# A delta-rule attention with an MoE behind it: fewer unread products, other banks at the start, and a moved Gram step

## The chip, the cores and the metric

The kernel runs on one core of one Trainium2 chip. A core has TensorE (PE) for matrix products, VectorE (DVE), ScalarE (ACT) and GpSimd (POOL) for elementwise work, and SyncE (SP), which here issues the loads and stores. Each engine takes its instructions in the order written and waits on semaphores for the others. The metric is the device time of one execution in microseconds, the median of several runs; lower is better.

## The reference

For each of 4 x 8 heads a state of 48 x 48 is updated over 768 positions, and the outputs of all heads, side by side, go through a two-layer network with a softplus:

```python
k_n = k / (norm(k) + 1e-6)
for t in range(768):
    y[t] = q[t] @ state
    state += beta[t] * outer(k_n[t], v[t] - k_n[t] @ state)
h = x @ w_in                      # x: 3072 x 384, w_in: 384 x 2048
out = softplus(h) @ w_out         # w_out: 2048 x 384
```

## The kernel before

The positions are cut into 12 chunks of 64. Inside a chunk the recurrence is a triangular system, so a chunk needs the Gram matrix of its keys (`gram`), the inverse of a triangular matrix made from it (`invert`), and products with the state. Two chunks share one inversion `u`. `invert(u)` transposes the Gram blocks on DVE, makes norms (`norms`: DVE, ACT's Ln and Exp, small pieces on POOL), multiplies by a column and a row (lines 325 and 327, the two products), and then runs a loop of 30 pairs of a product and an addition (lines 339 and 343), for inversions 1 to 5 on POOL. `finish(u)` transposes the result back on DVE (lines 346 and 349).

Chunks 0 and 1 are done in another way, so that the network can start early: their inverse is left in blocks of 16, and `couple(s)` multiplies the strict blocks with it; its two PSUM banks are emptied into three tiles of `MT`, the third of which is the second bank with its halves swapped. `base` gives x0, `sweep` adds the coupling three times. For chunk 0 this stands in the prologue, before the first product of the network; `first_mask`, `first_u` and `first_y` make its output. `pairs` hands out the banks for x0 and the sweeps. `warm` writes products that nobody reads; their operand is a constant tile, and line 813 is theirs.

The network runs in passes of one or two chunks, cut into steps `t`: in step `t` PE does `hidden(i, g)` (line 691: 2 tiles of 128 hidden units), ACT and DVE the softplus, and one step later PE does `output(i, g)` (line 737). Pass 0 uses 32-bit weights, later passes split weights and activations into a high and a low part (`high` on ACT, `low` on DVE). The weights come as raw halves and are put together by `top` (ACT) and `convert` (DVE, line 648).

The order around the network is written by hand. `plan` holds blocks of attention work for step `t` (run on PE behind `hidden(t)`) or `t + 0.5` (behind the `output` that follows). A step's code is written out for all engines at once, and each engine keeps that order. `start(u, solver, due)` puts an inversion into a background list, from which `pull` takes pieces at later steps, at the latest in step `due`. GRAM, END, DONE and INV give these steps: gram(4) at 4, gram(5) and the start of inversion 2 at 7, due at 11.

Transfers are issued by SP in the order of the calls. In the prologue `load_q(1)` comes after `first_y(1)`, since it overwrites q, and behind it `feed(20)`: 20 halves of weights. At step 0 follow the keys `ki(1)`, at step 1 v of chunk 2 and the transposed keys `kT` of chunk 4 (`load_v(2)`, `load_k(4)`), which gram(4) reads.

Of the kernel before, what the change touches and what calls it, by code (L numbers as in the profile page):

```python
# [7 lines left out]
F32 = mybir.dt.float32  # L8
# [13 lines left out]
P = 128  # L22
# [9 lines left out]
N16 = 1  # L32
# [8 lines left out]
PASS = {s: i for i, p in enumerate(PASSES) for s in p}  # L41

STEPS = {2: (8, 8.5, 9, 9.5, 10.5, 11, 11), 3: (11.5, 12, 13, 13, 13.5, 14, 14)}
CLEAR, DONE, END, GRAM, INV = {}, {1: 8, 2: 19}, {1: 6, 2: 17}, {4: 4, 5: 7}, {2: 11}
CLEAR.update({2: 9, 3: 12})
Q_FIRST = (2, 4, 5, 6, 7, 8, 9, 10)
for c in range(4, NS, 2):
# [13 lines left out]
def deltanet_moe(ctx, tc, kT, qT, kI, vN, beta, wts, out, outT):  # L61
# [14 lines left out]
    def bank(shape):  # L76
        turns[0] += 1
        if turns[0] % 4 == 0 and not both[0]:
            return ps_o.tile(shape, F32, name="po2")
        return ps_a.tile(shape, F32, name="pa")  # L80
# [62 lines left out]
        nc.sync.dma_start(NV[s], vN[s])  # L143

    def scale_v(s):
        (nc.vector if s > 1 else nc.gpsimd).tensor_tensor(NV[s], NV[s], NN[s].unsqueeze(2).to_broadcast([P, NP, D]),
                                op=ALU.mult)

    def parity(t):
# [139 lines left out]
    def diagonal(t, blocks, n, r0, c0, nr, nc_, wide=(True, True)):  # L289

        apart = n if t is Z else n * (HB + 1)
        dims = [t.ap[0]] + ([(apart, len(blocks))] if len(blocks) > 1 else [])
        dims += [(HB if wide[0] else 0, nr), (1 if wide[1] else 0, nc_)]
        return bass.AP(t.tensor, t.offset + r0 * HB + c0, dims)

    def invert(u):

        n = QB if u < N16 else HB  # L300
        blocks = range(0, HB, n)
        lq = one.tile([P, HB, HB], F32, name="ltq")
        nc.vector.transpose(lq, LTD[u].rearrange("p q i -> p i q"))  # L303
        yield 2200
        nm = norms(u, lq)
        next(nm)
        m = len(blocks)
        sq = diagonal(lq, blocks, n, 0, 0, n, n)
        for b in blocks:
            o = lq[:, b:b + n, b:b + n]  # L310
            nc.gpsimd.affine_select(
                out=o, in_=o, compare_op=ALU.is_gt, fill=0.0, base=0,
                pattern=[[1, n], [-1, n]], channel_multiplier=0)
        yield 300
        cT, ncT = yield from nm

        engine, cost = (nc.gpsimd, 0) if u in ON_POOL else (nc.vector, 1)
        if m > 1:
            by_col, by_row = (bass.AP(v.tensor, v.offset, [v.ap[0], (n, m)] + w) for v, w in
                              ((ncT, [(0, n), (1, n)]), (cT, [(1, n), (0, n)])))  # L320
        else:
            by_col = ncT.unsqueeze(1).to_broadcast([P, n, n])
            by_row = cT.unsqueeze(2).to_broadcast([P, n, n])
        first = engine if u == N16 else nc.vector
        first.tensor_tensor(sq, sq, by_col, op=ALU.mult)
        yield 200 + n * n * m
        first.tensor_tensor(diagonal(Z, blocks, n, 0, 0, n, n), sq, by_row, op=ALU.mult)
        yield 200 + n * n * m
        if m > 1:
            nc.gpsimd.tensor_copy(bass.AP(Z.tensor, Z.offset, [Z.ap[0], (n, m), (HB + 1, n)]),  # L330
                                  cT.rearrange("p (a b) -> p a b", b=n))
        else:
            engine.tensor_copy(Z.rearrange("p a b -> p (a b)")[:, 0:HB * HB:HB + 1], cT)
        for j in range(n - 2, 0, -1):
            r = n - 1 - j
            o = tmp[:, 0:m * r * j]
            o = (o.rearrange("p (a r j) -> p a r j", a=m, j=j) if m > 1
                 else o.rearrange("p (r j) -> p r j", j=j))
            engine.tensor_tensor(o, diagonal(Z, blocks, n, j + 1, j, r, j, (True, False)),  # L339
                                 diagonal(lq, blocks, n, j, 0, r, j, (False, True)),  # L340
                                 op=ALU.mult)
            z = diagonal(Z, blocks, n, j + 1, 0, r, j)
            engine.tensor_tensor(z, z, o, op=ALU.add)  # L343
            yield cost * 2 * (160 + m * r * j)
# [23 lines left out]
    def negative(engine, o, x):  # L368
        if engine is nc.scalar:
            engine.activation(o, x, AF.Copy, scale=-1.0)  # L370
        else:
            engine.tensor_scalar(o, x, -1.0, None, op0=ALU.mult)

    def couple(s):

        pms = [bank([P, NP // 2, C]) for e in range(2)]
        for i, e, p, ab, t in quads:
            nc.tensor.matmul(pms[e][tk[ab], i, :], LF[tk[t], s, p, :], DT[s][tk[t], p, :],
                             start=True, stop=True)
        negative(nc.scalar, MT[s][0], pms[0])  # L380
        negative(nc.scalar, MT[s][1], pms[1])
        for h in range(2):
            negative(nc.scalar, MT[s][2][tk[h]], pms[1][tk[1 - h]])

    def quarters(to, i0, n, flip, left, right, es=(0, 1), ends=None):

# [421 lines left out]
    def warm(*columns, behind=None):  # L808

        r = even if behind is None else behind  # L810
        to = unread[0] if unread else bank([P, 512])
        for m in columns:
            nc.tensor.matmul(to[:, 0:m], even[:, 0:P], r[:, 0:m], start=True, stop=True)  # L813

    with tc.manual_schedule(engines={ET.PE, ET.DVE, ET.Activation, ET.Pool, ET.SP}):
# [69 lines left out]
        warm(512)  # L885
        pts.append(first_p(1))
        run(iv)
        warm(512, 512)
        lq = one.tile([P, 2, NP // 2, C], F32, name="ltq")
        MT[0] = [lq[:, 0], lq[:, 1], two.tile([P, NP // 2, C], F32, name="gh")]  # L890
        warm(384, behind=Z.rearrange("p a b -> p (a b)"))
# [8 lines left out]
                [P, 8, D]), op=ALU.mult)  # L900
        for k in range(4):
            first_mask(k // 2, k % 2)
        couple(0)

        def pairs(g):
            return ([bank([P, 4, D]) for e in range(2)] if g == 0 else
                    [ps_h.tile([P, 4, D], F32, name=f"ph{e}") for e in range(2)])

        for g in range(2):
            i, to = slice(4 * g, 4 * g + 4), pairs(g)  # L910
            base(0, to, 4 * g, 4)
            nc.vector.tensor_copy(x_swap[:, i], to[1])
            nc.vector.tensor_copy(x_base[:, 0, i], to[0])
            for h in range(2):
                nc.gpsimd.tensor_copy(x_base[tk[h], 1, i], x_swap[tk[1 - h], i])
        warm(128)
        top()
        for b in range(C // QB):
# [12 lines left out]
        for g in range(2):  # L931
            sweep(0, 2, tos[g], 4 * g, 4, ends=(False, True))
            first_u(g, tos[g])
        warm(256)
        first_y(0)
        warm(256)
        first_y(1)
        load_q(1)
        both[0] = False
# [91 lines left out]
                                            op=ALU.add)  # L1031
            load_v(3)

        at(0, 6000, first_state, bind(steps, iv, 2))
        at(0.5, 0, bind(steps, iv, 2))
        at(1, 1200, bind(couple, 1), bind(scale_v, 1), bind(run, iv))
        at(2, 2400, bind(masked_keys, 1, 0))
        at(3, 2400, bind(masked_keys, 1, 1))
        at(4, 0, second_base)
# [12 lines left out]
        for c in range(2, NS, 2):  # L1052
            u = c // 2
            if STEPS[c][0] == STEPS[c + 1][0]:
                at(STEPS[c][0], 0, bind(cross_both, u, True))
                at(STEPS[c][1], 920, bind(cross_both, u, False), bind(scale_v, c + 1))
            else:
                for s in (c, c + 1):
                    at(STEPS[s][0], 0, bind(cross_a, s))
                    at(STEPS[s][1], 920 * (s - c), bind(cross_b, s),  # L1060
                       *([bind(scale_v, s)] if s > c else []))
            for s in (c, c + 1):
                a, b, k0, k1, v, y, z = STEPS[s]
                at(CLEAR[s], 0, bind(arrange, s))
                if c > 2:
                    at(k0, 2400, bind(all_keys, s))
                    at(k0 + 0.5, 0, bind(other_masks, s))
                    at(k0 + 1, 2400)
                    at(v, 0, bind(gram_and_corrected, s + 4, s) if s + 4 < NS else
                       bind(corrected, s))  # L1070
                    at(y, 1700, bind(state_and_y, s))
                    continue
                at(k0, 2400, *([bind(masked_keys, s, 0)] if k0 < k1 else []))
                at(k1, 2400, bind(masked_keys, s, *((1,) if k0 < k1 else (0, 1))))
                at(v, 0, bind(corrected, s))
                at(y, 1700, bind(y_all, s))
                if y == z:
                    at(y, 0, bind(next_state, s))
                else:
                    at(y, 0, bind(next_state, s, (0,)))  # L1080
                    at(z, 0, bind(next_state, s, (1,)))
            at(END[u], 0, bind(start, u, end, DONE[u]))
            if u > 2:
                if u == 3:
                    at(GRAM[c], 0, bind(load_beta, u), bind(systems, u), bind(gram_pair, c))
                at(8 * (c - 2) - (12 if u == 3 else EARLY), 0, bind(start, u, invert, INV[u]))
            elif u > 1:
                at(GRAM[c], 0, bind(load_beta, u), bind(systems, u), bind(gram, c))
                at(GRAM[c + 1], 0, bind(gram, c + 1), bind(start, u, invert, INV[u]))

        late, over = None, 0
        for t in range(8 * NS):
# [94 lines left out]
```

## Time and profile before

| | |
|---|---|
| median of 3 runs | 563.67 us (562.72 to 564.19) |
| profiled execution | 562.74 us, of it the span 561.0 us |
| PE matmul | 539.0 us busy (96%) |
| DVE, ACT | 367.2 and 363.9 us (65% each) |
| POOL | 209.6 us (37%) |
| granted clock of PE, mean | 0.988 |

The span is the time from the first to the last instruction; what the profiled execution took beyond it lies around the program. A busy engine is not the bound by itself: of interest is which engine is waited for last in a stretch. [...]

### The profile page before, as it was taken

The numbers are of one execution on the slowest core, as the hardware profiler recorded it, in microseconds if no ns is written. First come the engines' busy times: TensorE is split into PE (matmuls) and PEld (weight loads), VectorE is DVE, ScalarE is ACT, GpSimd is POOL, SyncE is SP. The second block draws the span as 40 slices with busy tenths as digits, with TensorE's granted clock in tenths as the row PEclk, the third lists the DMA queues.
The fourth block names the chain that finished last, engine by engine and source line by source line (L and its number), as shares of the span: only waits on it lengthen the run. The fifth ranks groups of instructions, "written<-read, shape, count | busy, mean of one in ns | idle before, by whom it ended". The sixth has DMA issues, their size and how long they took to land.

```text
span 561.0 us, 17602 instructions
## 1 busy us (share of the span) xinstructions
PE 539.0 (96%) x7479; PEld 443.0 (79%) x7479; DVE 367.2 (65%) x660; ACT 363.9 (65%) x719; POOL 209.6 (37%) x365
## 2 busy tenths in 40 slices
PE   5788999899999999999999999999999999999997
PEld 3476768699987888877888888888887888888885
DVE  7858966999757857368747378747375737444434
ACT  5668685898677874756773757754557754454453
POOL 7125898119980179701886001886000000000000
PEclk9699999999999999999999999999999999999999
DMA  9919911223240132220122220031310030010001
GB/s 201 330 49 373 315 38 32 72 58 86 58 90 2 32 72 57 72 85 4 30 70 60 70 89 3 3 81 29 77 71 4 1 71 2 15 57 0 2 0 57
DMA packets 35502, 39.56 MB, mean 71 GB/s; under 512 B 22528, under 2 KB 25216, under 8 KB 35424
## 3 DMA queue, kind: packets, MB, share of 16 engines
q1 hardware_dynamic: 35280, 38.18, 24.2%
q8 instruction: 59, 0.97, 0.7%
q10 hardware_dynamic: 144, 0.26, 0.1%
q14 instruction: 19, 0.16, 0.1%
HBM read 31.55 MB, written 4.72 MB: 65 GB/s over the span
## 4 chain that ended last, share of the span: by engine, by line
PE 69%; POOL 16%; DVE 7%; DMA 3%; issue 2%; ACT 2%; ACTq 0%; DVEq 0%; POOLq 0%
PE po L737 29%; PE ph L691 27%; POOL Z L343 7%; POOL tmp L339 7%; PE pa L596 3%; PE pa L479 2%; DMA kt<-kT 2%; PE pa L439 2%; PE pa L565 1%; DMA big<-qT 1%; PE po L813 1%; DVE tt L349 1%; PE ph L577 1%; PE pa L577 1%; DVE a L668 1%
## 5 line engine op out<-in xcount | busy, mean ns | idle before, releaser
L691 PE MATMUL ph<-x,b 128*128 128x512 f32 (+1 forms) x576 | 166.2, 373 | 0.0
L696 ACT ACTIVATE a<-ph 128x512 f32<-128x512 f32 x96 | 57.4, 598 | 157.8 <-PE ph L691 153.2
L691 PE MATMUL ph<-x,a 128*128 128x512 f32 (+1 forms) x384 | 129.6, 374 | 2.4 <-DVE a L648 1.8
L703 DVE SCALAR_TENSOR_TENSOR a<-ph,a 128x512 f32<-128x512 f32 x88 | 60.4, 687 | 93.5 <-ACT a L698 93.2
L691 PEld LDWEIGHTS ph<-x,b 128*128 128x128 f32 x576 | 105.0, 188 | 19.4
L737 PE MATMUL po<-gh,b 128*128 128x512 f32 (+1 forms) x241 | 97.6, 405 | 1.4 <-DVE gh L705 1.4
L737 PE MATMUL po<-gh,a 128*128 128x512 f32 (+1 forms) x241 | 94.1, 390 | 0.0
L343 POOL TENSOR_TENSOR Z<-Z,tmp 128x30 f32<-128x30 f32 (+9 forms) x150 | 89.6, 597 | 11.8
L339 POOL TENSOR_TENSOR tmp<-Z,ltq 128x30 f32<-128x30 f32 (+9 forms) x150 | 86.5, 576 | 11.4
L691 PEld LDWEIGHTS ph<-x,a 128*128 128x128 f32 x384 | 72.0, 189 | 15.6 <-DVE a L648 2.2
L706 DVE TENSOR_TENSOR gl<-a,gh 128x512 fp32r<-128x512 f32 x88 | 66.4, 754 | 7.9 <-DVE gh L705 0.5
L737 PE MATMUL po<-gl,b 128*128 128x512 f32 (+1 forms) x241 | 69.4, 389 | 0.0
L698 ACT ACTIVATE a<-a 128x512 f32<-128x512 f32 x96 | 60.7, 632 | 3.1
L697 ACT ACTIVATE a<-a 128x512 f32<-128x512 f32 x96 | 60.6, 632 | 3.1
L737 PEld LDWEIGHTS po<-gh,b 128*128 128x128 f32 x241 | 45.2, 187 | 12.7 <-DVE gh L705 1.9
L737 PEld LDWEIGHTS po<-gl,b 128*128 128x128 f32 x241 | 45.2, 188 | 9.6
L737 PEld LDWEIGHTS po<-gh,a 128*128 128x128 f32 x241 | 45.3, 188 | 8.5
L705 DVE CAST gh<-a 128x512 fp32r<-128x512 f32 x88 | 40.0, 454 | 8.1 <-DVE a L703 0.9
L602 DVE TENSOR_TENSOR x<-pa,x 128x384 fp32r<-128x384 f32 x21 | 11.6, 554 | 38.1 <-ACT x L601 38.1
L256 POOL COPY ss<-ltq 128x32 f32<-128x32 f32 x6 | 1.4, 241 | 86.8 <-DVE ltq L303 86.8
L737 PE MATMUL po<-a,gh 128*128 128x384 f32 x96 | 33.5, 444 | 0.3 <-DVE gh L709 0.3
L493 DVE TENSOR_TENSOR big<-pa,maskP 64x256 f32<-64x256 f32 x66 | 27.8, 421 | 1.0
(220 smaller groups left out, 752.8 us busy)
## 6 DMA issues: line engine op xcount, KB each, us to landing
a<-wts SPq DMA_DIRECT2D x16, 383.8 KB, 7.5
b<-wts SPq DMA_DIRECT2D x16, 383.8 KB, 7.4
kt<-kT SPq DMA_DIRECT2D x24, 192.0 KB, 3.4
big<-qT SPq DMA_DIRECT2D x24, 192.0 KB, 4.0
nv<-vN SPq DMA_DIRECT2D x12, 384.0 KB, 3.7
ki<-kI SPq DMA_DIRECT2D x24, 192.0 KB, 3.3
outT<-ot SPq DMA_DIRECT2D x13, 256.0 KB, 2.3
x<-x SPq DMA_DIRECT2D x66, 32.0 KB, 2.0
```

What stands on the lines that cost most here:

```text
L339: engine.tensor_tensor(o, diagonal(Z, blocks, n, j + 1, j, r, j, (True, False)), diagonal(lq, blocks, n, j, 0, r, j, (False, True)), op=AL ...
L343: engine.tensor_tensor(z, z, o, op=ALU.add)
L493: nc.vector.tensor_tensor(be[tk[ab], ab, e, 4 * g:4 * g + 4, 0:C], pks[e][t, :, 0:C], maskP[t].unsqueeze(1).to_broadcast([C, 4, C]), op=AL ...
L596: nc.tensor.matmul(py[tk[ab], i, :], big[:, at + C:at + 2 * C], big[:, at:at + C], start=True, stop=True)
L691: nc.tensor.matmul(ph[:, j], weight(i, f, a, k * P, P), xr[b][k], start=(c == 0), stop=(c == len(terms) * NK - 1))
L696: nc.scalar.activation(a, ph, AF.Abs)
L697: nc.scalar.activation(a, a, AF.Exp, scale=-1.0)
L698: nc.scalar.activation(a, a, AF.Ln, bias=1.0)
L703: nc.vector.scalar_tensor_tensor(a, ph, 0.0, a, op0=ALU.max, op1=ALU.add)
L705: nc.vector.tensor_copy(hi_lo[0], a)
L706: nc.vector.tensor_tensor(hi_lo[1], a, hi_lo[0], op=ALU.subtract)
L737: nc.tensor.matmul(PO[i][h][:, c], l, r, start=(fs[j] == 0 and m == 0), stop=(fs[j] == NF - 1 and m == k - 1 and c != (cut and parts[0])))
```

## The change

It takes away three unread products and shortens a fourth; gives x0 and the sweeps of chunk 0 the banks of `ph` and `po` instead of `pa` and `ph`; lets DVE empty the second bank of couple(0) and puts the third copy behind x0; puts one copy of x0 on ACT; puts the two products of inversion 1 and the scaling of v(1) on DVE, the latter behind the products; puts two pieces of inversion 1 ahead of the first state; and in the tables puts gram(4) at 3.5 and the start of inversion 2 at 8.5.

```diff
--- before.py
+++ after.py
@@ -41,7 +41,7 @@
 PASS = {s: i for i, p in enumerate(PASSES) for s in p}
 
 STEPS = {2: (8, 8.5, 9, 9.5, 10.5, 11, 11), 3: (11.5, 12, 13, 13, 13.5, 14, 14)}
-CLEAR, DONE, END, GRAM, INV = {}, {1: 8, 2: 19}, {1: 6, 2: 17}, {4: 4, 5: 7}, {2: 11}
+CLEAR, DONE, END, GRAM, INV = {}, {1: 8, 2: 19}, {1: 6, 2: 17}, {4: 3.5, 5: 7}, {2: 11}
 CLEAR.update({2: 9, 3: 12})
 Q_FIRST = (2, 4, 5, 6, 7, 8, 9, 10)
 for c in range(4, NS, 2):
@@ -143,7 +143,7 @@
         nc.sync.dma_start(NV[s], vN[s])
 
     def scale_v(s):
-        (nc.vector if s > 1 else nc.gpsimd).tensor_tensor(NV[s], NV[s], NN[s].unsqueeze(2).to_broadcast([P, NP, D]),
+        nc.vector.tensor_tensor(NV[s], NV[s], NN[s].unsqueeze(2).to_broadcast([P, NP, D]),
                                 op=ALU.mult)
 
     def parity(t):
@@ -321,10 +321,9 @@
         else:
             by_col = ncT.unsqueeze(1).to_broadcast([P, n, n])
             by_row = cT.unsqueeze(2).to_broadcast([P, n, n])
-        first = engine if u == N16 else nc.vector
-        first.tensor_tensor(sq, sq, by_col, op=ALU.mult)
+        nc.vector.tensor_tensor(sq, sq, by_col, op=ALU.mult)
         yield 200 + n * n * m
-        first.tensor_tensor(diagonal(Z, blocks, n, 0, 0, n, n), sq, by_row, op=ALU.mult)
+        nc.vector.tensor_tensor(diagonal(Z, blocks, n, 0, 0, n, n), sq, by_row, op=ALU.mult)
         yield 200 + n * n * m
         if m > 1:
             nc.gpsimd.tensor_copy(bass.AP(Z.tensor, Z.offset, [Z.ap[0], (n, m), (HB + 1, n)]),
@@ -378,9 +377,12 @@
             nc.tensor.matmul(pms[e][tk[ab], i, :], LF[tk[t], s, p, :], DT[s][tk[t], p, :],
                              start=True, stop=True)
         negative(nc.scalar, MT[s][0], pms[0])
-        negative(nc.scalar, MT[s][1], pms[1])
-        for h in range(2):
-            negative(nc.scalar, MT[s][2][tk[h]], pms[1][tk[1 - h]])
+        negative(nc.scalar if s else nc.vector, MT[s][1], pms[1])
+
+        def rest():
+            for h in range(2):
+                negative(nc.scalar, MT[s][2][tk[h]], pms[1][tk[1 - h]])
+        return rest
 
     def quarters(to, i0, n, flip, left, right, es=(0, 1), ends=None):
 
@@ -885,7 +887,6 @@
         warm(512)
         pts.append(first_p(1))
         run(iv)
-        warm(512, 512)
         lq = one.tile([P, 2, NP // 2, C], F32, name="ltq")
         MT[0] = [lq[:, 0], lq[:, 1], two.tile([P, NP // 2, C], F32, name="gh")]
         warm(384, behind=Z.rearrange("p a b -> p (a b)"))
@@ -900,19 +901,20 @@
                 [P, 8, D]), op=ALU.mult)
         for k in range(4):
             first_mask(k // 2, k % 2)
-        couple(0)
+        rest = couple(0)
 
         def pairs(g):
-            return ([bank([P, 4, D]) for e in range(2)] if g == 0 else
-                    [ps_h.tile([P, 4, D], F32, name=f"ph{e}") for e in range(2)])
+            return [(ps_o, ps_h)[g == 0].tile([P, 4, D], F32, name=f"{'po' if g else 'ph'}{e}")
+                    for e in range(2)]
 
         for g in range(2):
             i, to = slice(4 * g, 4 * g + 4), pairs(g)
             base(0, to, 4 * g, 4)
             nc.vector.tensor_copy(x_swap[:, i], to[1])
-            nc.vector.tensor_copy(x_base[:, 0, i], to[0])
+            copies[g](x_base[:, 0, i], to[0])
             for h in range(2):
                 nc.gpsimd.tensor_copy(x_base[tk[h], 1, i], x_swap[tk[1 - h], i])
+        rest()
         warm(128)
         top()
         for b in range(C // QB):
@@ -931,9 +933,8 @@
         for g in range(2):
             sweep(0, 2, tos[g], 4 * g, 4, ends=(False, True))
             first_u(g, tos[g])
-        warm(256)
+        warm(192)
         first_y(0)
-        warm(256)
         first_y(1)
         load_q(1)
         both[0] = False
@@ -1031,9 +1032,8 @@
                                             op=ALU.add)
             load_v(3)
 
-        at(0, 6000, first_state, bind(steps, iv, 2))
-        at(0.5, 0, bind(steps, iv, 2))
-        at(1, 1200, bind(couple, 1), bind(scale_v, 1), bind(run, iv))
+        at(0, 6000, bind(steps, iv, 2), first_state, bind(steps, iv, 2))
+        at(1, 1200, lambda: couple(1)(), bind(run, iv), bind(scale_v, 1))
         at(2, 2400, bind(masked_keys, 1, 0))
         at(3, 2400, bind(masked_keys, 1, 1))
         at(4, 0, second_base)
@@ -1086,7 +1086,8 @@
                 at(8 * (c - 2) - (12 if u == 3 else EARLY), 0, bind(start, u, invert, INV[u]))
             elif u > 1:
                 at(GRAM[c], 0, bind(load_beta, u), bind(systems, u), bind(gram, c))
-                at(GRAM[c + 1], 0, bind(gram, c + 1), bind(start, u, invert, INV[u]))
+                at(GRAM[c + 1], 0, bind(gram, c + 1))
+                at(8.5, 0, bind(start, u, invert, INV[u]))
 
         late, over = None, 0
         for t in range(8 * NS):
```

On PE, around steps 3 and 4, `ph` rows are the network's hidden products, `po_1026` and `po_1023` its outputs, `kt_74` the transposed keys of chunk 4, `nv` the products of second_base. Before:

```order
L737 MATMUL po_1027<-a_138,gh 128x384
L691 MATMUL ph_1134<-x_89,a_783 128x256 x3
L691 MATMUL ph_1134<-x_89,a_787 128x256 x3
L393 MATMUL pa<-nv,tt 64x48 x32
L192 MATMUL po_1190<-kt_74 64x64 x2
L192 MATMUL pa<-kt_74 64x64 x2
...
L737 MATMUL po_1026<-a_775,gh 128x384
```

and in the changed kernel:

```order
L739 MATMUL po_1024<-a_138,gh 128x384
L192 MATMUL pa<-kt_74 64x64 x32
L693 MATMUL ph_1177<-x_89,a_780 128x256 x3
L693 MATMUL ph_1177<-x_89,a_784 128x256 x3
L395 MATMUL po_1192<-nv,tt 64x48 x2
L395 MATMUL pa<-nv,tt 64x48 x2
...
L739 MATMUL po_1023<-a_772,gh 128x384
```

The Gram products of chunk 4 stood behind hidden(0, 4) and second_base and now stand ahead of both, directly behind output(0, 2).

On DVE, between the last weight part of step 7 (`a_1566`, `a_1563`) and the next step, `ltq<-work` is the transpose that begins inversion 2, `r`, `nt`, `ncT` and `nn` its norms, and `a<-ph` the softplus of step 8. Before:

```order
L668 TENSOR_TENSOR a_1566<-a_130,b_1503 128x768
L303 STREAM_TRANSPOSE ltq<-work 128x1024
L257 TENSOR_SCALAR rt<-ltq 128x32
L261 RECIPROCAL r_1603<-rt 128x32
L262 TENSOR_TENSOR r_1603<-r_1603,ss 128x32
L263 SCALAR_TENSOR_TENSOR nt<-r_1603,rt 128x32
L265 TENSOR_TENSOR r_1603<-nt 128x32
L266 RECIPROCAL r_1603<-r_1603 128x32
L269 SCALAR_TENSOR_TENSOR ncT<-r_1603,bet 128x32
L279 STREAM_TRANSPOSE nn<-nt 128x32
L285 TENSOR_SCALAR nn<-nn 128x32
L703 SCALAR_TENSOR_TENSOR a<-ph_1576,a 128x512
```

and in the changed kernel:

```order
L670 TENSOR_TENSOR a_1563<-a_130,b_1500 128x768
L705 SCALAR_TENSOR_TENSOR a<-ph_1573,a 128x512
L707 CAST gh<-a 128x512
L708 TENSOR_TENSOR gl<-a,gh 128x512
L670 TENSOR_TENSOR a_1638<-a_134,b_1502 128x768
L670 TENSOR_TENSOR a_1640<-a_138,b_1569 128x768
L670 TENSOR_TENSOR a_1642<-a_772,b_1571 128x768
L303 STREAM_TRANSPOSE ltq<-work 128x1024
L257 TENSOR_SCALAR rt<-ltq 128x32
L485 TENSOR_TENSOR nv<-nv,pa 128x4x48
```

The transpose stood ahead of the softplus of step 8 and now stands behind it and behind three weight parts; the norms follow later still, directly ahead of the two products of inversion 2, which keep their place ahead of the softplus of step 10.

## Rows read from the trace of the kernel before

**Rows 1.** The page's 40 slices: granted clock of PE, in tenths

```profile
PEclk9699999999999999999999999999999999999999
```

**Rows 2.** PE's waits: releaser, us in total, times, longest

```profile
PE ph L691 <- DVE a L648: 1.8, 1, 1.8
```

**Rows 3.** Timeline of the prologue: start us, us, engine, line, operation, tiles

```profile
25.05 0.92 ACT L364 ACTIVATE tt<-tmp,blk 128x256 f32<-128x256 f32 x2
25.42 1.98 PE L813 MATMUL po<-gl 128*128 128x512 f32 x4
27.98 1.16 PE L378 MATMUL pa<-tt,x 64*64 64x64 f32 x64
29.24 1.09 ACT L370 ACTIVATE ltq<-pa 128x512 f32<-128x512 f32 x2 [3.27 <-PE pa L378]
30.34 1.20 ACT L370 ACTIVATE gh<-pa 64x512 f32<-64x512 f32 x2
31.58 0.68 PE L393 MATMUL pa<-x,ltq 64*64 64x48 f32 x32
...
38.30 0.70 PE L813 MATMUL po<-gl 128*128 128x256 f32 x2
40.45 2.86 PE L691 MATMUL ph<-x,a 128*128 128x256 f32 x12 [0.60 <-ACT x L546]
```

**Rows 4.** SP's issues; loads from 38 to 76 us; us to landing from 61.1

```profile
39.87 1.31 SPq L135 DMA_DIRECT2D big<-qT  x2
61.20 4.18 SPq L127 DMA_DIRECT2D kt<-kT  x4
...
DMA packets 5301, 10.31 MB, mean 271 GB/s; under 512 B 2160, under 2 KB 2160, under 8 KB 5296
...
kt<-kT SPq DMA_DIRECT2D x1, 192.0 KB, 9.8
```

**Rows 5.** Timeline of PE around steps 3 and 4

```profile
66.38 2.75 PE L691 MATMUL ph<-x,a 128*128 128x256 f32 x12
...
71.18 0.30 PE L192 MATMUL po<-kt 48*64 48x64 f32 x2 [0.97 <-DMA kt<-kT]
...
72.90 2.85 PE L737 MATMUL po<-a,gh 128*128 128x384 f32 x8
```

**Rows 6.** PE's timeline, then stretches (PEclk: third from the end)

```profile
7.49 0.68 PE L177 MATMUL po<-kt 48*64 48x64 f32 x31
19.70 2.58 PE L192 MATMUL pa<-kt 48*64 48x64 f32 x64 [2.88 <-DMA kt<-kT]
...
11.00:11.50 0.50, 0.00 (x0) 0.00 (x0) 0.50 (x1) 0.00 (x0) 0.00 (x0) 0.89 1.33 246
25.00:25.50 0.50, 0.50 (x33) 0.43 (x25) 0.50 (x3) 0.50 (x3) 0.00 (x0) 0.96 1.04 418
```

**Rows 7.** Timeline of POOL and DVE, products of inversion 1 and a conversion

```profile
51.48 2.67 POOL L325 TENSOR_TENSOR ltq<-ltq,ncT 128x1024 f32<-128x1024 f32 x1
...
51.85 2.70 DVE L648 SCALAR_TENSOR_TENSOR a<-a,ex 128x384 int32<-128x384 int32 x1
57.26 0.54 DVE L648 SCALAR_TENSOR_TENSOR a<-a,ex 128x384 int32<-128x384 int32 x1
```

**Rows 8.** Timeline of ACT and DVE, steps 8 to 10

```profile
103.64 0.63 ACT L698 ACTIVATE a<-a 128x512 f32<-128x512 f32 x1
...
103.58 1.95 DVE L303 STREAM_TRANSPOSE ltq<-work 128x1024 f32<-128x1024 f32 x1
106.31 0.35 DVE L261 RECIPROCAL r<-rt 128x32 f32<-128x32 f32 x1 [0.56 <-ACT rt L259]
108.53 0.68 DVE L703 SCALAR_TENSOR_TENSOR a<-ph,a 128x512 f32<-128x512 f32 x1
121.75 1.23 DVE L327 TENSOR_TENSOR Z<-ltq,cT 128x1024 f32<-128x1024 f32 x1
```

**Rows 9.** Timeline of POOL and PE: end of loop 2, wait behind finish(2)

```profile
166.91 0.27 POOL L343 TENSOR_TENSOR Z<-Z,tmp 128x30 f32<-128x30 f32 x1
...
173.15 0.50 PE L737 MATMUL po<-gh,b 128*128 128x512 f32 x1 [0.56 <-DVE gh L705]
```

## The prediction

> **What bounds the kernel now.** The page comes first: PE fills its slices and its clock is up from 28 us on [rows 1], so time can be won only where PE stands still or does work that nobody reads. The table of PE's waits shows where it stands, behind weight conversions on DVE above all [rows 2], behind late keys and a few copies. I then read the timeline in PE's order, because PE takes its work strictly as written and hands a late start on to all that follows.
>
> In the first 40 us PE, ACT and DVE work as a chain. The coupling runs at 27.98, its last copy is out of ACT only at 31.54, the first sweep starts at 31.58, and the first MoE product, after ACT's copy of y, at 40.45 [rows 3]. From 40 us on a second thing runs: a stream of loads. SP starts it at 39.87 when the last first_y has read q, and the keys of chunk 4 stand at its end: issued at 61.20, landed 9.8 us later, about 71.0 [rows 4]. PE asks for them at 71.18 after waiting 0.97 us [rows 5]. After that PE hardly waits until 173.15, where gh is late by 0.56 us [rows 9]: gh stands behind finish(2) on DVE, and that behind the last step of POOL's second loop, at 167.18 (166.91 + 0.27). So two things set the end: when the keys of chunk 4 arrive, and when POOL's second loop starts.
>
> **The prologue.** Without the two unread 512-wide products, couple(0) waits only for ACT's masks, which end at 25.97 (25.05 + 0.92) [rows 3], and for the unread product behind Z, which then ends near 26.2: couple starts 1.8 us earlier. Its two halves are then emptied side by side: ACT takes 0.55 (half of 1.09) [rows 3]. DVE has no row for such a copy; the nearest are ACT's 0.55 and its own softplus, as wide and also out of PSUM, 0.68 [rows 8]. I take 0.68; one mask that is late on DVE would add 0.5. The third copy (1.20) moves behind x0, and since x0 and the sweeps have other banks, its bank no longer holds the first sweep. That sweep then starts near 28.7 (couple done at 27.3, DVE's copy, behind its masks, until 28.3, a copy of x0 0.35) instead of 31.58: 2.9 us. Before first_y(1) an unread 256-wide product of 0.70 goes [rows 3]; the copy of u on ACT hides some of it, which leaves 0.45. Sum: the first MoE product, and with it the start of the load stream, comes 3.3 us earlier (36.5 for the stream). Bounds 1.8 (only the unread product counts) and 3.9.
>
> **The second inversion's start.** Its two 1024-wide products on POOL took up to 2.67 us, and one of DVE's conversions beside them took 2.70 instead of about 0.55 [rows 7]; PE waited 1.8 us for a conversion [rows 2]. On DVE they are two instructions like the later inversion's 1.23 [rows 8], and they now stand behind those conversions. So PE's wait of 1.8 goes, and 0.3 of the following wait for gh. POOL's first loop starts about 6 us earlier; PE and DVE reach the place where it is read later than it ends, so those 6 us are slack and count nothing. The same holds for scale_v(1) on DVE (0.9): DVE has room there because its conversions are no longer stretched; if that cover went, keys(1) would be 0.9 late.
>
> **gram(4) moved ahead.** PE used to end output(0, 2) at 66.38 [rows 5]. With 3.3 + 1.8 + 0.3 taken off it ends at about 61.0, and now the next thing in PE's row is gram(4), which needs the keys. These come with the stream. SP's order of loads is unchanged, the weights before the keys keep the engines full, so the keys shift by the stream's start only: 71.0 - 3.3 = 67.7. PE therefore stands still for 6.7 us (bounds 5.5 and 7.5). Behind gram(4) wait hidden(0, 4), second_base and output(0, 3); ACT, DVE and POOL have nothing that can use the time.
>
> What is then late: before, gram took from 71.18 to 72.90 (1.72) and output(0, 3) followed; hidden(0, 4) and second_base, 3.83 us (71.18 - 0.97 - 66.38), were already done [rows 5]. Now they come after the keys. Shift at the start of output(0, 3) (72.90 before): -3.3 + 3.8 = +0.5 us. The whole prologue gain and the removed waits are spent here.
>
> **The clock.** PE's long run ends at 8.17 in the first gram; with only a fraction of a microsecond of work in between, the granted clock goes from 1.00 to 0.50 in the slice from 11.00, and it is back in the slice from 25.00, after PE worked from 19.70 on [rows 6]. [...] A stop of 6.7 us is longer than what went before that fall, so I expect PE to restart at the low level. If it stays there as long as from 19.70 to 25.02, 5.3 us, gram takes 2.58 as it did there instead of 1.72, 0.9 more, and hidden(0, 4) loses half of the 2.7 that are left, 1.3: together 2.2. Bounds 0 (no fall) and 3.5 (7 us at the low level). I take 2.2. The shift is then +2.7 at output(0, 3), and PE, which hardly waited from there to step 8, carries it along.
>
> **The third inversion's start.** Before, DVE did its transpose from 103.58 and its norms until 108.53, then softplus(8) and all else, and the second product ended at 122.98 (121.75 + 1.23) [rows 8]. So ACT's end of softplus(8), 104.27, stood 18.7 before the loop. Now softplus(8) and three weight parts come first, and transpose and norms later, in the same row of DVE: 14.45 (122.98 - 108.53) plus the 4.95 that were between 103.58 and 108.53, less the wait for ACT in it, 0.56 [rows 8], is 18.84, some 18.9 from ACT's end. DVE idles before ACT's end instead of using that time. Costs 0.2, bounds 0 and 0.8. That ACT no longer holds cross_a's copies behind the logarithm saves PE about 1.6 at step 8, but PE only arrives earlier at the wait of 173.15; this counts nothing.
>
> **The sum.** POOL's second loop starts -3.3 + 3.8 + 2.2 + 0.2 = +2.9 us later. Its length (44.2, from 122.98 to 167.18) I leave, with 1 us either way for DVE's traffic. finish(2) follows at once, PE waits for it, and everything behind shifts by 2.9. The profiled execution took 562.74 (span 561.0 and 1.74 around it), so 565.6 on its account; it lies 0.9 below the median of 563.67, so the median of the runs should be 566.5.
>
> [...] The stream's length is the step on which all hangs. The trace has 10.31 MB at a mean of 271 GB/s from 38 to 76 us [rows 4], and PE waited for its end.
> [...]
>
> **The rivals.** *The keys don't hold PE* (12%). If keys and PE arrive together at 61, PE is 6.4 us early at output(0, 3) (72.90 against 61.0 + 1.72 + 3.83 = 66.5), POOL's second loop starts at most 5.8 earlier (finish(1) and the steps behind it on DVE take the rest): 557.9. It takes a stream that ends at 61; the result turns at about 66.6 with the clock up (where -3.3 + 3.8 + 0.2 becomes 0). For it: the last megabyte moves at half the rate of the weights, so there is room. Against it: nothing in that part of the queue is changed, and the issue of each load waits for the eighth before it.
>
> *PE stops but its clock stays up, or comes back at once* (20%). Then +0.7: 564.4, no change that can be told. For it: PE stood 1.8 us in one place [rows 2] and the clock row shows 9 in every slice from 28 us on [rows 1]. Against: 6.7 us is nearly four times that, and the fall in rows 6 came 3.3 us after the last long run.
>
> *The clock falls in the prologue too* (8%). The unread products are what fills PE between 25.4 and 40; if one of the new gaps lets the clock fall there, the small products of about 10 us run at half rate, some 4 us later, and the stream with them: 570.5. For it: three stretches of filling go. Against: the chain gets shorter by as much, and no gap of over 1 us opens.
>
> *The forecast* (60%): 566.5, own range 565 to 568.5.
>
> **Numbers.** A measurement of this kernel can't tell less than 0.3%, 1.7 us, from no change. Faster: the first rival, and a little of the second, 0.13. Same: most of the second and the low end of the forecast, 0.27. Slower: 0.60. The range from 562.0 to 569.5 leaves out the first rival and half of the third.
>
> **What would show it.** In the changed profile: couple(0) near 26.2 and the first MoE product near 37.1; no long conversions beside POOL; PE idle about 6.7 us before gram's first product, released by the key load; granted clock 0.50 for about five us after it; POOL's second loop starting near 125.9; PE waiting over 2 us for gh at about 176. I am wrong if PE finds the keys landed, if the clock stays at 1.00, or if the wait at finish(2) isn't there.

## The result and the profile after the change

The changed kernel takes 568.16 us, median of six executions (566.1 to 569.59), where the kernel before took 563.22 on the same chip: ratio 1.0083, 95% interval 1.0058 to 1.0108, so 4.9 us slower by the medians and 4.7 by the ratio. The forecast was 566.5, 2.8 above the median it started from. The profiled execution has a span of 567.1 us, before 561.0. Its checkpoints, in us from the span's start:

| | before | forecast | after |
|---|---|---|---|
| couple(0) starts | 27.98 | 26.2 | 26.14 |
| first sweep | 31.58 | 28.7 | 30.70 |
| first MoE product | 40.45 | 37.1 | 40.02 |
| stream of loads starts | 39.87 | 36.5 | 39.39 |
| gram(4) gets its keys | 71.18 | 67.7 | 69.78 |
| PE's wait just before | 0.97 | 6.7 | 5.68 |
| output(0, 3) starts | 72.90 | 75.6 | 78.06 |
| third inversion's second product done | 122.98 | 125.9 | 128.07 |
| PE's product behind finish(2) | 173.15 | 176 | 179.03 |

The prologue comes first: the timeline of the changed kernel, its PE, ACT, DVE and SP rows (columns as in [rows 3] and [rows 4]).

```profile
26.14 1.16 PE L377 MATMUL pa<-tt,x 64*64 64x64 f32 x64
27.39 0.60 ACT L369 ACTIVATE ltq<-pa 128x512 f32<-128x512 f32 x1 [1.62 <-PE pa L377]
27.41 0.68 DVE L371 TENSOR_SCALAR ltq<-pa 128x512 f32<-128x512 f32 x1
27.57 0.51 PE L395 MATMUL po<-nv,tt 64*64 64x48 f32 x18
29.91 0.44 PE L395 MATMUL po<-nv,tt 64*64 64x48 f32 x14 [1.83 <-issue]
30.70 0.68 PE L395 MATMUL ph<-x,ltq 64*64 64x48 f32 x32
40.02 2.86 PE L693 MATMUL ph<-x,a 128*128 128x256 f32 x12 [0.57 <-ACT x L548]
39.39 1.31 SPq L135 DMA_DIRECT2D big<-qT  x2
60.33 4.40 SPq L127 DMA_DIRECT2D kt<-kT  x4
```

Coupling, and its emptying by two engines, came as forecast, to 0.2 us, the DVE copy at the 0.68 that was taken for it. Then base's second half stops after 18 of its 32 products for 1.83 us, and the releaser is "issue": no semaphore that the profile knows. Of the 3.3 us of the forecast 0.4 reach the first MoE product.

PE around the keys of chunk 4, which answers to [rows 5]:

```profile
61.25 2.85 PE L739 MATMUL po<-a,gh 128*128 128x384 f32 x8
69.78 2.46 PE L192 MATMUL pa<-kt 48*64 48x64 f32 x64 [5.68 <-DMA kt<-kT]
72.16 4.89 PE L693 MATMUL ph<-x,a 128*128 128x256 f32 x12
78.06 2.85 PE L739 MATMUL po<-a,gh 128*128 128x384 f32 x8
```

Three stretches of the same kernel (bounds, length, busy time of PE, PEld, DVE, ACT, POOL, then granted clock as a share of PE's full speed, DMA share, GB/s):

```profile
30.00:35.00 5.00, 5.00 (x156) 4.32 (x158) 2.74 (x10) 2.12 (x6) 0.69 (x2) 0.69 0.03 7
65.00:70.00 5.00, 0.23 (x2) 0.26 (x2) 3.94 (x6) 0.00 (x0) 4.53 (x7) 0.95 0.88 210
70.00:75.00 5.00, 4.97 (x71) 4.12 (x71) 0.00 (x0) 2.62 (x8) 4.45 (x8) 0.50 0.03 8
```

PE stands still for the keys, and the granted clock behind that is 0.50: gram takes 2.46 us and hidden(0, 4) 4.89. It was down in the prologue too: two us after the stop in base it fell, and from 32 to 34 us it was 0.50.

The third inversion and the end of its loop, on ACT, DVE and POOL, and PE behind it (these answer to [rows 8] and [rows 9]):

```profile
108.79 0.63 ACT L700 ACTIVATE a<-a 128x512 f32<-128x512 f32 x1
109.45 0.69 DVE L705 SCALAR_TENSOR_TENSOR a<-ph,a 128x512 f32<-128x512 f32 x1 [4.58 <-ACT a L700]
114.10 2.07 DVE L303 STREAM_TRANSPOSE ltq<-work 128x1024 f32<-128x1024 f32 x1
126.84 1.23 DVE L326 TENSOR_TENSOR Z<-ltq,cT 128x1024 f32<-128x1024 f32 x1
133.70 0.74 PE L418 MATMUL pa<-tt,off 32*32 32x32 f32 x64 [1.97 <-DVE x L606]
172.07 0.27 POOL L342 TENSOR_TENSOR Z<-Z,tmp 128x30 f32<-128x30 f32 x1
179.03 0.50 PE L739 MATMUL po<-gh,b 128*128 128x512 f32 x1
```

From ACT's end of softplus(8), 109.42, to the second product's end are 18.65 us, where 18.9 was forecast. POOL's second loop starts and ends 5.1 us late, and PE's product behind it 5.9. The long wait for gh that was expected at 176 is missing: PE itself came late, since it waited 1.97 us at 131.7 for a bank that DVE empties behind the norms of the third inversion.

### The profile page after: what moved, and what is told of

It is laid out like the page before. It is cut to its first block, busy times and chain, and to the rows that moved or that the text cites. A ratio compares the mean times of both kernels' runs of the same rounds, so it can differ in the third digit from the quotient of the medians.

```text
span 567.1 us, 17588 instructions
## 1 busy us (share of the span) xinstructions
PE 542.2 (96%) x7473; PEld 446.5 (79%) x7473; DVE 365.4 (64%) x663; ACT 363.6 (64%) x719; POOL 202.6 (36%) x362
## 4 chain that ended last, share of the span: by engine, by line
PE 85%; DMA 6%; DVE 3%; ACT 2%; SPq 1%; issue 1%; POOL 1%; ACTq 0%; DVEq 0%; POOLq 0%
PE po L739 33%; PE ph L693 33%; PE pa L598 4%; DMA kt<-kT 3%; DMA b<-wts 3%; PE pa L481 2%; PE pa L441 2%; PE pa L567 2%; PE pa L579 1%; PE pa L192 1%; PE ph L579 1%; PE ph L241 1%; PE po L395 1%; PE po L815 1%; DMA big<-qT 1%
## 5 line engine op out<-in xcount | busy, mean ns | idle before, releaser
L693 PE MATMUL ph<-x,a 128*128 128x512 f32 (+1 forms) x384 | 132.1, 383 | 0.6 <-ACT x L548 0.6
L693 PEld LDWEIGHTS ph<-x,b 128*128 128x128 f32 x576 | 106.3, 191 | 19.4
L338 POOL TENSOR_TENSOR tmp<-Z,ltq 128x30 f32<-128x30 f32 (+9 forms) x150 | 85.0, 567 | 11.4
L693 PEld LDWEIGHTS ph<-x,a 128*128 128x128 f32 x384 | 74.2, 194 | 13.9 <-ACT x L548 0.7
```

Source lines behind the costliest of these rows:

```text
L693: nc.tensor.matmul(ph[:, j], weight(i, f, a, k * P, P), xr[b][k], start=(c == 0), stop=(c == len(terms) * NK - 1))
```

## The experiments

Each ratio is to the kernel before, run on the same chip (its medians were 563.0 to 563.2).

| kernel | us | ratio | 95% interval |
|---|---|---|---|
| the change | 568.16 | 1.0083 | 1.0058 to 1.0108 |
| a_gram_behind | 565.59 | 1.0045 | 1.0031 to 1.0059 |
| b_gram_ahead | 566.35 | 1.0058 | 1.0044 to 1.0071 |
| a_fill | 565.93 | 1.0060 | 1.0036 to 1.0083 |
| a_keys_early | 559.66 | 0.9942 | 0.9926 to 0.9957 |
| a_warm_kept | 567.69 | 1.0082 | 1.0061 to 1.0102 |
| a_keys_feed_less | 558.01 | 0.9914 | 0.9901 to 0.9928 |
| a_inv3_at7 | 565.01 | 1.0042 | 1.0027 to 1.0057 |
| a_pool_products | 567.69 | 1.0084 | 1.0062 to 1.0107 |
| best7 | 558.02 | 0.9918 | 0.9898 to 0.9938 |
| b_keys_feed_less | 562.38 | 0.9992 | 0.9979 to 1.0005 |

The ratio is not the quotient of the two medians. a_gram_behind_2 and a_inv3_at7_2 are single executions of the kernels that they are named after, taken for their traces: 565.52 and 566.09 us.

**gram(4)'s place, both ways.** In the changed kernel it goes back; in the kernel before it alone goes ahead.

```diff
-{4: 3.5, 5: 7}
+{4: 4, 5: 7}      # a_gram_behind, a_gram_behind_2
-{4: 4, 5: 7}
+{4: 3.5, 5: 7}    # b_gram_ahead
```

> The changed kernel with gram(4) back behind hidden(0,4) and second_base. Theory (late keys plus the fallen clock are the loss): PE ends output(0,2) near 64.1, has 3.8 us of hidden(0,4) and second_base to do, waits some 2 us for keys that land near 69.8, gram takes 1.7 at a granted clock of 1.00, and output(0,3) starts near 71.6 instead of 78.06: about 562, 6 us less than the change. Rival (the loss comes from the later start of the third inversion or from the products on DVE): still 567 to 568.

> The changed kernel with gram(4) back behind hidden(0,4) and second_base once more, for its trace; five executions took 565.6, where 562 was expected. If PE still comes to the keys 2 us early and runs on at 71.6 with the clock up, what holds the end is not PE but something that starts at its own time, the first POOL loop or the third inversion behind softplus(8). If PE starts output(0,3) at 74 or later, it was held again, by the clock or by a bank.

> The kernel before with one edit only, gram(4) ahead of hidden(0,4) and second_base. Theory: PE comes to gram(4) at 66.4, waits 4.6 us for keys that land at 71.0, and has hidden(0,4) and second_base (3.8 us) behind it; output(0,3) starts at 76.5 if the clock stays up (566.9 in all), at 78.7 to 79.5 if it falls to 0.50 as in the changed kernel (569 to 570). Rival (the place of gram(4) is not what costs): 563, as before.

The kernel before loses 3.2 us by that one edit, although the clock falls, with which 569 to 570 was expected; part of the rest is taken up on DVE (below, at the third inversion). Its PE:

```profile
71.37 2.35 PE L192 MATMUL pa<-kt 48*64 48x64 f32 x64 [4.88 <-DMA kt<-kT]
73.65 4.58 PE L691 MATMUL ph<-x,a 128*128 128x256 f32 x12
79.23 2.85 PE L737 MATMUL po<-a,gh 128*128 128x384 f32 x8
```

Wait, half clock (0.53 from 70 to 75 us) and order are those of the change, in a kernel that has nothing else of it. By the ratios the way back gave 2.1 us of the 4.7, not the 6 that I expected. Its SP rows, PE rows and clock show why:

```profile
38.28 1.31 SPq L135 DMA_DIRECT2D big<-qT  x2
...
70.59 0.95 PE L192 MATMUL po<-kt 48*64 48x64 f32 x3 [3.93 <-DMA kt<-kT]
...
73.19 4.56 PE L739 MATMUL po<-a,gh 128*128 128x384 f32 x8
...
70.00:75.00 5.00, 4.26 (x67) 3.35 (x68) 0.00 (x0) 1.72 (x5) 4.44 (x7) 0.50 0.13 39
```

The keys came at 70.59 though the stream began at 38.28, and a wait of 3.93 us lowered the clock as well; output(0, 3) ran at the low level in its turn. From SP's issue of q to gram's first product are 32.3 us here, 30.4 in the change, 31.3 before: the stream's length varies by 2 us, and what makes it vary is open.

**Work in the place of the wait.** Six unread 512-wide products directly ahead of gram(4).

```diff
+            to = ps_o.tile([P, 512], F32, name="po2")
+            for _ in range(6):
+                nc.tensor.matmul(to, even[:, 0:P], even, start=True, stop=True)
-                at(GRAM[c], 0, bind(load_beta, u), bind(systems, u), bind(gram, c))
+                at(GRAM[c], 0, bind(load_beta, u), bind(systems, u), fill, bind(gram, c))
```

> The changed kernel with six unread 512-wide products on PE directly ahead of gram(4), some 5.1 us of work in the place of the 5.7 us stop; nothing starts earlier or later because of them. Theory (part of the loss is the clock): the granted clock stays at 1.00 behind the keys, gram takes 1.7 instead of 2.45 and hidden(0,4) 2.7 instead of 4.9: 2.9 us less, about 565. Rival (gram and hidden(0,4) are slow for another reason, the loads or DVE): 568, as the change.

```profile
63.69 5.39 PE L1047 MATMUL po<-gl 128*128 128x512 f32 x12 [0.48 <-DVE big L495]
69.50 1.62 PE L192 MATMUL pa<-kt 48*64 48x64 f32 x64 [0.42 <-DMA kt<-kT]
71.05 2.86 PE L693 MATMUL ph<-x,a 128*128 128x256 f32 x12
74.91 2.85 PE L739 MATMUL po<-a,gh 128*128 128x384 f32 x8
...
70.00:75.00 5.00, 5.00 (x139) 4.29 (x139) 0.00 (x0) 3.74 (x10) 4.45 (x8) 1.00 0.02 5
```

The keys come 0.3 us earlier than in the change, the granted clock from 70 to 75 us is 1.00 instead of 0.50, and from there to output(0, 3) PE needs 5.41 us instead of 8.28. So the fallen clock alone costs 2.87 us in this place. The median fell by 2.2, by the ratios it is 1.3 and the two intervals overlap, so it is the trace that carries this.

**The keys ahead of the weights.** Nothing reads the buffer kt0 after the second first_p, so the load may stand earlier.

```diff
         load_q(1)
+        load_k(4)
         both[0] = False
...
                         load_v(2)
-                        load_k(4)
```

> The changed kernel with the load of the keys of chunk 4 issued ahead of the 20 weight loads instead of behind them. Theory: keys land before 48, gram(4) finds them, PE does not stop, the clock stays at 1.00, output(0,3) starts near 69.7 instead of 78.06, and the end comes up to 8.4 us earlier, about 560. Rival 1 (the weights, now 2 us later, hold PE's first MoE products in their place): 562 to 563. Rival 2 (the loss is elsewhere): 568.

It takes 559.66. PE's row, and one of DVE:

```profile
64.53 1.16 PE L192 MATMUL pa<-kt 48*64 48x64 f32 x64
...
69.49 2.85 PE L739 MATMUL po<-a,gh 128*128 128x384 f32 x8
...
95.56 2.00 DVE L345 STREAM_TRANSPOSE tt<-Z 128x1024 f32<-128x1024 f32 x1 [4.63 <-POOL Z L342]
```

No wait; gram takes 1.16, and output(0, 3) starts 8.6 us earlier than in the change. The weights behind the keys hold nobody. What holds the end now is POOL's first loop: DVE waits 4.63 us for it, until 95.56.

**The prologue.** One kernel puts the unread products back; another, on top of the early keys, moves three of the twelve early weight loads behind the coupling.

```diff
         run(iv)
+        warm(512, 512)     # a_warm_kept
...
-        feed(6)
+        feed(3)            # a_keys_feed_less, with the early keys
-        feed(20)
+        feed(23)
```

> The changed kernel with the two unread 512-wide products ahead of lq put back. Theory (their removal was worth nothing, because PE then stands for 1.8 us in base): base starts near 29.9 without a stop, the first MoE product stays near 40.0, the granted clock between 30 and 35 is 1.00, and the time is within 0.5 us of the change, 568. Rival (they cost their 1.8 us): first MoE product near 41.8, 570.

> The kernel with the keys of chunk 4 loaded ahead of the weights (559.7), and three of the twelve weight loads of the prologue moved behind those keys. Theory (PE's stop of 1.7 to 1.8 us in base, released by nothing the profile shows, is PE's own instructions that come in behind the weight loads): the loads end near 26, the stop goes, the first MoE product comes near 38.3 and the end 1.7 us earlier, 558. Rival (the stop comes with the instructions whatever the loads do): it stays at 1.7 and the time at 559.7, or above it where the weights, three loads later, hold hidden(0,2).

With the unread products kept the time is the change's within its interval, so taking them out was worth nothing that these runs can tell, to about 1 us. The checkpoints were not those expected: base stops, for 0.59 us, and the first MoE product comes at 38.41. Part of that lead is this execution's own, since its clock was up earlier (0.66 from 22 to 24 us, where the change had 0.50). With fewer early loads the stop is gone, and the time is 1.6 us below that of a_keys_early (the intervals just touch):

```profile
27.48 0.99 PE L395 MATMUL po<-nv,tt 64*64 64x48 f32 x32
...
37.64 2.86 PE L693 MATMUL ph<-x,a 128*128 128x256 f32 x12 [0.57 <-ACT x L548]
```

What the DMA queues moved from 27 to 28 us (packets, MB, share of 16 engines), in the change and then in this kernel:

```profile
q1 hardware_dynamic: 151, 0.41, 101.6%
q8 instruction: 1, 0.02, 5.8%
```

```profile
q1 hardware_dynamic: 3, 0.01, 1.6%
```

In the change the loads fill every engine while a packet of a queue called "instruction" passes between them; PE stands still soon after. With the loads out of the way by 27 us the same products run through. My reading is that PE waited for its own instructions behind the weights. That the packet is PE's, no row says, but the place of the stop speaks for it. In a_warm_kept, with two unread products (four in PE's rows) more ahead of it, the stop stands behind 14 of the 32 products instead of 18:

```profile
28.98 0.55 PE L395 MATMUL po<-nv,tt 64*64 64x48 f32 x18 [0.59 <-issue]
```

Counted along PE's row (in the change 474 products, 474 weight loads and 13 semaphore and drain instructions), the stop stands behind number 961 in all seven traces that have it. A second stop, of 0.41 us, stands behind number 1217, just 256 further, in a_gram_behind_2, a_keys_early and a_keys_feed_less, where the loads had ended. Each of these stops ends 2.3 to 2.6 us after a packet of the instruction queue begins (27.63 to 29.91 in the change, 26.58 to 28.97 in a_warm_kept). The change brings PE to number 961 at 28.08 instead of 30.5, but the packet passes when it did before (27.63, before 27.71). With fewer loads it passes at 25.80.

**The third inversion's place, and the products.**

```diff
-                at(8.5, 0, bind(start, u, invert, INV[u]))
+                at(7, 0, bind(start, u, invert, INV[u]))    # a_inv3_at7, a_inv3_at7_2; best7 with early keys and fewer early loads
...
+        first = engine if u == N16 else nc.vector           # a_pool_products
-        nc.vector.tensor_tensor(sq, sq, by_col, op=ALU.mult)
+        first.tensor_tensor(sq, sq, by_col, op=ALU.mult)
```

(and the second product likewise)

> The changed kernel with the third inversion's start back at step 7, so that its transposition and norms stand ahead of softplus(8) on DVE again. DVE stood idle for 4.58 us there. Theory (the later place costs once PE is late): the transposition starts near 105.6 behind ACT's copies of gram(5), the norms wait for ACT until 109.9, softplus(8) starts near 111.9, and POOL's loop starts near 126.4 instead of 128.3: 1.9 us less, about 566.3. Rival (the prediction's step: both orders hang on ACT's end of softplus(8) and differ by 0.2): 568.

> The changed kernel with the third inversion's start at step 7 once more, for its trace; its executions took 565.0, 2.3 us less than the change by the ratios. Theory: transposition near 105.6 and ahead of softplus(8), DVE idle 2 us for ACT in the norms instead of 4.58, second product done near 126.4 where the change has 128.07. If it is done at 128 all the same, the 2.3 us come from elsewhere.

The place costs the change 2.3 us by the ratios. DVE's row with the start at step 7:

```profile
105.79 2.10 DVE L303 STREAM_TRANSPOSE ltq<-work 128x1024 f32<-128x1024 f32 x1 [0.64 <-ACT work L200]
...
110.13 0.35 DVE L261 RECIPROCAL r<-rt 128x32 f32<-128x32 f32 x1 [2.02 <-ACT rt L259]
...
125.31 1.23 DVE L326 TENSOR_TENSOR Z<-ltq,cT 128x1024 f32<-128x1024 f32 x1
```

The transposition fills part of what was 4.58 us of idle time, and the second product ends at 126.54 instead of 128.07, though PE started output(0, 3) 0.3 later here (78.36). PE's wait of 1.97 for the bank is gone too. Taken back singly, the places of gram(4) and of the third inversion are worth 2.1 and 2.3 of the 4.7 us; both at once, with the keys late, was not run.

> The changed kernel with the two products of the second inversion back on POOL (their norms and the order stay). Theory (the 6 us that the first POOL loop starts earlier are slack while the keys hold PE): conversions take up to 2.7 us beside POOL again, PE waits about 1.8 us for one and as much less for the keys (3.7 instead of 5.7), the first POOL loop ends near 97 and DVE still comes to it later (98.8): 568, as the change. Rival (the earlier loop was worth something): 570.

567.69, the change's time. The products took 2.37 and 2.11 us on POOL and the two conversions beside them 2.15 and 2.09, PE waited 0.6 for a conversion and 5.08 for the keys, and DVE came to finish(1) at 97.30 without a wait for POOL. As expected, except that the loop ended at 93.2 and not near 97: the norms, which the change also moved ahead, let it start early wherever the products run. Here it starts at 52.14, in the change at 54.21, since on DVE the products stand behind four conversions.

> The kernel with early keys and fewer early weights (558.0) and the third inversion's start at step 7 as well. Theory (without a late PE, DVE comes to the end of the first POOL loop too early and waits for it in either order, so the order is worth little): 557.5, within 0.7 us of 558.0. Rival (the order is worth the 2.3 us that it was worth in the change): 555.7.

> The kernel before with only the two edits to SP's row: keys of chunk 4 ahead of the weights, three weight loads of the prologue behind them. Theory (without late keys the kernel before is held by its first POOL loop, which starts at 56.8 behind conversions and products on POOL): PE's wait for keys of 0.97 goes, the loop still ends near 97, and the time is 562 to 563; then the original change is worth 4 to 5 us once the keys are early. Rival (the gain is all the keys'): 558 to 559.

With the keys early the order of step 7 or 8.5 makes no difference (558.02 against 558.01). The kernel before with the same two SP edits stays where it was, 562.38. DVE at the end of the first POOL loop, first of that kernel, then of a_keys_feed_less:

```profile
96.84 1.95 DVE L346 STREAM_TRANSPOSE tt<-Z 128x1024 f32<-128x1024 f32 x1 [3.54 <-POOL Z L343]
```

```profile
92.63 1.97 DVE L345 STREAM_TRANSPOSE tt<-Z 128x1024 f32<-128x1024 f32 x1 [4.09 <-POOL Z L342]
```

Both wait for that loop, and 4.2 us lie between them, about the 4.4 us between the two times: 2.2 from the shorter prologue (first MoE product at 37.64 against 39.81), the rest from the earlier start of the second inversion. Whether it is the norms' place or the products' that gives this rest was not run with early keys. a_keys_feed_less, 0.9% below the kernel before, is the version to keep.

## Why the prediction was right, and which steps of it were not

The time came out 4.9 us slower where 2.8 was forecast. Where the steps below were off in the sum, they were off the same way, so the errors add up.

**Right: what decides.** gram(4) moved ahead makes PE stand at the keys (5.68 us), the clock falls to its low level (0.50), and the third inversion starts late by all of it. b_gram_ahead shows the first two alone, a_fill the clock, a_keys_early that without late keys the loss turns into a gain. The first rival took the slow last megabyte of the stream for room; there was none. Between 66 and 69 us of the changed kernel the engines were 99% busy and moved 228 GB/s, while the weights went at 416 (52 to 59 us), and the keys came at 69.78. In the first rival the turning point should be keys at 67.0 (67.7 less the 0.7), not 66.6; nothing hangs on it.

**Wrong: the prologue's term.** The step "the first MoE product, and with it the start of the load stream, comes 3.3 us earlier" gave 0.4 to 0.5. The chain behind the coupling was not bound by the copies alone: base was cut by the stop of 1.83, where PE, brought there sooner, in my reading ran out of instructions. Before, base came later, and the only wait in it was one of 0.65, put down to ACT. Moved loads take the stop away, and the first MoE product then comes 2.8 us earlier (37.64). Most of the rest was the clock at 0.69 from 30 to 35 us, the third rival's mechanism. From the end of the stop to the first MoE product the traces of this prologue take 9.34 us with the clock up (a_fill, a_pool_products) and 10.11 and 10.48 with it down (the change, a_inv3_at7_2): it costs 0.8 to 1.1 us, not 4, and does not happen in every execution. Why not is open. By this step the keys came 1.4 us earlier instead of 3.3, and 1.9 us of the shift at output(0, 3) that the forecast lacks are this.

**Mis-sized: the clock.** 2.2 was taken, for 5.3 us at the low level; a_fill measures 2.87. The granted clock was still 0.50 from 75 to 76 us, so the low level lasted over 6 us behind the keys, and all of hidden(0, 4) ran at it.

**Wrong in its meaning: the third inversion's place.** "Costs 0.2" measured the distance from ACT's end of softplus(8), and that distance held. But before, ACT's end was not what DVE waited for: it stood 3.5 us for POOL's first loop, and ACT was done 4.3 us before DVE came to softplus(8) [rows 8]. DVE behind that loop, first before, then in the change, and the second product of b_gram_ahead:

```profile
97.58 1.95 DVE L346 STREAM_TRANSPOSE tt<-Z 128x1024 f32<-128x1024 f32 x1 [3.54 <-POOL Z L343]
...
98.82 1.95 DVE L345 STREAM_TRANSPOSE tt<-Z 128x1024 f32<-128x1024 f32 x1
...
126.20 1.23 DVE L327 TENSOR_TENSOR Z<-ltq,cT 128x1024 f32<-128x1024 f32 x1
```

The old place would have taken up part of PE's delay, and the new one hands on all of it: b_gram_ahead, late by 6.3 us at output(0, 3), ends its second product only 4.45 late, at 127.43. Between the two places are 1.5 us in the traces (the second product of a_inv3_at7_2 against the change's) and 2.3 by the ratios. The sum was right for the new place, the price of the edit was not.

**Right by luck: the products.** The earlier first loop was slack in the changed kernel, as forecast. But it starts only 2.6 us earlier (54.21 against 56.77), not about 6, since POOL waits there for the products on DVE; and the reason given, that it ends before anyone wants it, is true only behind the late keys. The kernel before did wait for it, for 3.5 us, which stands in DVE's waits and not in PE's, by which the prediction went.

**Not seen:** the wait at finish(2), whose absence the prediction named as a sign of being wrong. In this step it was: PE's arrival, and not POOL's loop, was the last limit there. gh was there at 178.25 and PE at 179.03, because the bank wait at 131.7, with the clock at 0.72 in the 5 us after 135, had made PE itself late. Two limits ended within 0.8 us of each other, so PE's product came 3.0 us later than forecast: 2.2 by which the second product was later (128.07 against 125.9), and these 0.8.

## What to carry to other kernels

Ask of every step that is moved ahead what it reads and when that lands: here PE, in its fixed order, gave back at the keys all that was won before them, and the stop of 5.68 us cost 2.87 more in the clock behind it. Price an edit against the engine that waits last now: in the kernel before, DVE's wait of 3.5 us for POOL's first loop hid what the third inversion's place costs once PE comes late. And when a change fails on one late transfer, try that transfer's place in its queue before the change is dropped: here two edits to SP's row turned 4.9 us of loss into 5 us of gain, while in the kernel before they were worth nothing that can be told.

## What the hardware showed that was not expected

PE stopped for 1.2 to 1.8 us in the middle of one loop of equal products with no releaser, in six traces with the weight loads of the prologue beside it, and for 0.6 us in a_warm_kept, where the packet of the instruction queue passed a microsecond earlier (26.58 against 27.63). In the change that packet is 0.02 MB, and the 256 instructions from number 961 to number 1217 are 127 products, as many weight loads and two semaphore instructions. That PE stood for its own instructions there is my reading; the traces show the packet, the stop and its place.

The granted clock fell to 0.50 after a stop of 3.93 us as after one of 5.68. In the change it also fell after stops of 1.83 us (in base; 0.50 from 32 to 34) and 1.97 us (for the bank at 131.7; 0.72 from 135 to 140), each time when PE was already at work again; after a stop of 1.74 us in a_keys_early it stayed at 1.00 (30 to 35).
